# Windowed attention and two MLPs on one core: the opening's weight work behind the attention rows, a scale step tied to its join, and one wide block a gap earlier

## The chip, the cores and the metric

The kernel runs on one core of a Trainium2 chip. TensorE (PE) multiplies matrices, ScalarE (ACT) and VectorE (DVE) read its results and write its operands, GpSimd (POOL) and SyncE (SP) issue transfers, and POOL also computes a little. Each engine works through its own list of instructions in the order in which the program wrote them. The metric is the device time of one execution in microseconds (us).

## The reference, cut to what matters

```python
# windowed attention: B=4, H=8, S=768, D=64; 8 memory rows in k and v
for c in range(S // 32):                       # chunks of 32 queries
    k_full = concat([mem_k, k[l_start:r_end]]) # window: 16 left, 32, 8 right
    scores = scale * q_c @ k_full.T ; a = softmax(scores)
    out[chunk] = a @ concat([mem_v, v[l_start:r_end]])
x = out as 3072 tokens x 512
# first MLP:   h = x @ w_in (512 x 2048); g = max(0.01*h, h); y = g @ w_out
# second MLP:  h = y @ w_in2; P = a0 + a1 h + a2 h^2 + a3 h^3
#              Q = 1 + |b0||h| + |b1| h^2; out = (P / (Q + 1e-6)) @ w_out2
```

The MLP inputs come as 64-bit floats. The kernel reads each as two 32-bit words, joins them to one 32-bit float, and multiplies in split form: a number is a high half and a low half, and a product is three matmuls (high by high, high by low, low by high).

## The kernel before, in words

Tokens go in six tiles of 512 through each MLP layer. The middle dimension of 2048 is cut into 16 slices of 128, so each layer has 96 items (tile, slice). An item is 12 matmuls into a bank `hps` (`emit_h`, L596, three for each of four pieces of the inner dimension), an eviction on ACT that applies the leaky function twice (`gh` L606, `s` L607), a subtraction on DVE (`gl`, L609), and 12 matmuls into `acc` (`emit_y`, L654). A round c of the main loop first emits `hps` of item c+3 and its eviction, then the `acc` matmuls of item c; attention work stands in the two gaps behind these. So the eviction `gh` of item n is followed on PE by the `acc` matmuls of item n-3 and then by `hps` of item n+1.

A weight slice comes as a "half": one for `w_in` ("i") and one for `w_out` ("o") of each slice, in the order i0, i1, i2, o0, i3, o1, i4 and so on. A half goes through a load (SP, L121 or L124), a scale (ACT, L133), a join (three DVE instructions L147, L150, L154) and a split: a cast to the high half `wih` or `woh` (ACT, L165) and the low half `wil` or `wol` (DVE, L168, called `lower`). While the first tile is multiplied, `weights0` does this twice in a round: its first call stands behind `gh` and `s` of the round and has `gl` put into the middle of its join, its second call stands in the second gap. Three raw buffers `wr` hold loaded halves.

In the opening, the eight attention blocks of the first tile go through stages that overlap: `att_a` (transposes of q and k on PE, copies on ACT), `att_b1` (scores `pss` and their maxima `mx` on DVE), `att_e` (exp on ACT), `att_b2` (sum, reciprocal, scaling `pm` on DVE), `att_c` (transposes `pst`, copies `pb` on ACT) and `att_d` (`psx`, then `xh` on ACT and `xl` on DVE). The second tile's eight blocks are cut into pieces that `attend` spreads over the rounds of the first tile; their exp is four instructions with a row sum (L324). The later tiles use a wider form of block with a plan of slots (`wide_plan`, two slots a round). No scheduler reorders anything; the order of the code is the order on each engine.

Of the kernel before, what the change touches and what calls it, by code (L numbers as in the profile page):

```python
# [16 lines left out]
P = 128  # L17
QB = 64
LCTX, RCTX, CHUNK = 16, 8, 32
# [5 lines left out]
def kernel(  # L25
# [23 lines left out]
    nc = tc.nc  # L49
    B, H, S, D = q.shape  # L50
    NM = mem_k.shape[2]
# [118 lines left out]
    def weights0(between=()):  # L170
        if n_split[0] < FC * 2:
            lower = split_w()
            scale_w(FC * 2)
            join_w(FC * 2, between)
            lower()
            load_w(FC * 2)
        else:
            for fn in between:
                fn()
# [47 lines left out]
    qr, qT, kT, pm = {}, {}, {}, {}  # L227
    in_mem = {}

    def load_kv(j, src, mem, kind, spans):  # L230
        bi, blk = divmod(j, BPS)
        t = rooms[kind][place(kind, j)]
        c0 = blk * QB - LCTX
        for row, at, n, is_mem in spans:
            if is_mem:
                if in_mem.get((kind, place(kind, j), row)) != bi:
                    in_mem[kind, place(kind, j), row] = bi
                    nc.sync.dma_start(out=t[row:row + n], in_=mem[bi].rearrange("h p d -> p h d"))  # L238
            else:
                lo, hi = max(c0 + at, 0), min(c0 + at + n, S)  # L240
                row += lo - c0 - at
                nc.sync.dma_start(out=t[row:row + hi - lo], in_=src[bi, :, lo:hi, :].rearrange("h p d -> p h d"))
# [4 lines left out]
        nc.sync.dma_start(out=t, in_=q[bi, :, blk * QB:blk * QB + P, :].rearrange("h p d -> p h d"))  # L247
        qr[j] = t

    def load_k(j):  # L250
        load_kv(j, k, mem_k, "k", ((0, 0, NM, True), (NM, 0, CTX, False), (NM + CTX, 0, NM, True)))

    def load_qk(j):
        if j >= NB:
            return
        if j % 2 == 0:
            load_q(j)
        load_k(j)

    def load_v(j):  # L260
        if j < NB:
            W = WIN - NM
            load_kv(j, v, mem_v, "v", ((0, 0, NM, True), (NM, 0, W, False),
                                       (SB, CHUNK, W, False), (SB + W, 0, NM, True)))

    def att_bank(j, name):

# [254 lines left out]
    def wide_plan():  # L522
        def put(slot, *fns):
            wide_at.setdefault(slot, []).extend(fns)
        n0 = WIDE_FROM * NMAX // P
        last = NT // P - 1
        base = 2 * FC * (WIDE_FROM - 1)
        at = {j: base - 7 + 8 * (j - n0) for j in range(n0, last + 1)}
        at[n0], at[n0 + 1], at[n0 + 2] = base - 4, base + 3, base + 10
        put(at[n0] - 7, lambda: wide_load_qk(n0))  # L530
        put(at[n0] - 5, lambda: wide_q(n0), lambda: wide_k(n0))
        put(at[n0] - 4, lambda: wide_qk(n0), lambda: wide_load_qk(n0 + 1))
        for j in range(n0, last + 1):
            u = at[j]
            put(u, lambda j=j: wide_s(j))
            put(u + 1, lambda j=j: wide_e(j))
            if j < last:
                put(u + 1, lambda j=j: wide_q(j + 1))
                put(u + 2, lambda j=j: wide_k(j + 1))
                put(u + 3, lambda j=j: wide_qk(j + 1))  # L540
            put(u + 3, lambda j=j: wide_n(j), lambda j=j: wide_load_v(j))
            put(u + 4, lambda j=j: wide_p(j))
            put(u + 5, lambda j=j: turn_in(2, j, pwT))
            put(u + 6, lambda j=j: wide_load_qk(j + 2))
            put(u + 10, lambda j=j: wide_x(j))

    def wide(slot):
        for fn in wide_at.get(slot, ()):
# [154 lines left out]
    with tc.manual_schedule():  # L703
# [3 lines left out]
        nc.vector.memset(vb[0][0:32], 0.0)  # L707
        nc.gpsimd.memset(pall, 0.0)
        load_qk(0)
        nc.vector.memset(lnb, ONE * 2.0 ** -LN_SHIFT)  # L710
        nc.vector.memset(expb, -LN_SHIFT * math.log(2.0))
        load_k(1)
        load_v(0)
        load_qk(2)
        load_w(FC * 2)
        load_v(1)
        load_k(3)
        load_w(FC * 2)
        load_v(2)
        load_q(4)  # L720
        load_v(3)
        att_a(0)
        load_k(4)

        for j in range(FIRST + 2):
            if j < FIRST:
                att_b1(j)
                if j + 1 < FIRST:
                    att_a(j + 1)
                    if j + 5 < FIRST:  # L730
                        load_k(j + 5)
                    if j == 1:
                        load_q(6)
                att_e(j)
                att_b2(j)
            if 1 <= j <= FIRST:
                att_c(j - 1)
            if j >= 2:
                att_d(j - 2)
                if j + 2 < FIRST:  # L740
                    load_v(j + 2)
            if j == 3:
                load_w(FC * 2)
                scale_w(FC * 2)
                scale_w(FC * 2)
                join_w(FC * 2)
            if j == 4:
                load_w(FC * 2)
            if j in (5, 7, 8, 9):
                weights0()  # L750
            if j == FIRST:
                load_qk(FIRST)
                load_qk(FIRST + 1)
            if j == FIRST + 1:
                load_v(FIRST)
                load_v(FIRST + 1)
                nc.sync.dma_start(out=coef[:, 0:4], in_=a.partition_broadcast(P))
                nc.sync.dma_start(out=coef[:, 4:6], in_=b.partition_broadcast(P))

        issued_h = [0]  # L760

        def advance_h(upto):
            while issued_h[0] < min(upto, len(items)):
# [12 lines left out]
                if issued_h[0] == len(items):  # L776
                    rational(c + 1, False, True)

        wide_plan()
        advance_h(LA)  # L780
        weights0()
        for c in range(len(items)):
            layer, i, f = items[c]
            if layer == 0:
# [17 lines left out]
            if layer == 0 and i + 1 < WIDE_FROM:  # L802
                n0, n1 = tiles_of[0][i + 1]
                lastb = (n0 + n1) // QB - 1
                firstb = n0 // QB
                p0, p1 = block_end.get(firstb - 1, 0), block_end[lastb]
                span = FC - LA - 2
                start = p0 + (p1 - p0) * min(2 * f + 1, 2 * span) // (2 * span)
                end = p0 + (p1 - p0) * min(2 * f + 2, 2 * span) // (2 * span)
            look = LA if c + LA < NA else LB  # L810
            early = f == FC - 1
            if not early:
# [59 lines left out]
```

## Time and profile before

| | |
|---|---|
| median of 3 runs | 1165.43 us (1165.14 to 1165.69) |
| the profiled execution | 1165.79 us, span 1164.0 us |
| mean granted TensorE clock | 0.994 |
| busy: PE, DVE, ACT, POOL | 1135.2, 776.6, 637.2, 222.6 us |
| PE's sequence of `hps` starts | item 0 at 47.68 us |

The span is the time from the first to the last instruction in the trace; the execution is 1.79 us longer. A timeline row has the start, the duration, the engine, the line, the operation, the tiles, and in brackets how long the engine sat idle before it and what ended that.

### The profile page before, as it was taken

The numbers are of one execution on the slowest core, as the hardware profiler recorded it, in microseconds if no ns is written. First come the engines' busy times: TensorE is split into PE (matmuls) and PEld (weight loads), VectorE is DVE, ScalarE is ACT, GpSimd is POOL, SyncE is SP. The second block draws the span as 40 slices with busy tenths as digits, with TensorE's granted clock in tenths as the row PEclk, the third lists the DMA queues.
The fourth block names the chain that finished last, engine by engine and source line by source line (L and its number), as shares of the span: only waits on it lengthen the run. The fifth ranks groups of instructions, "written<-read, shape, count | busy, mean of one in ns | idle before, by whom it ended". The sixth has DMA issues, their size and how long they took to land.

```text
span 1164.0 us, 19701 instructions
## 1 busy us (share of the span) xinstructions
PE 1135.2 (98%) x7552; PEld 927.8 (80%) x7552; DVE 776.6 (67%) x1388; ACT 637.2 (55%) x1195; POOL 222.6 (19%) x255
## 2 busy tenths in 40 slices
PE   6699999999999999999999999999999999999998
PEld 4577778878887887888888888888888888888887
DVE  3788865555455554554234888788788788788775
ACT  4577742223223223223344877777777777777765
POOL 0000121132112231121000222222222222222222
PEclk9799999999999999999999999999999999999999
DMA  8677797879777787852432200200200200200000
GB/s 177 152 186 199 178 243 190 220 221 244 196 207 226 201 220 205 229 156 69 134 127 91 91 1 1 73 1 1 73 1 1 73 1 1 73 1 1 37 1 37
DMA packets 148593, 132.00 MB, mean 113 GB/s; under 512 B 63416, under 2 KB 119064, under 8 KB 148500
## 3 DMA queue, kind: packets, MB, share of 16 engines
q1 hardware_dynamic: 143635, 123.30, 37.8%
q0 software_dynamic: 4864, 7.45, 2.9%
q8 instruction: 60, 0.98, 0.4%
q14 instruction: 34, 0.27, 0.1%
HBM read 92.93 MB, written 37.75 MB: 112 GB/s over the span
## 4 chain that ended last, share of the span: by engine, by line
PE 92%; ACT 2%; DVE 2%; DMA 2%; SPq 1%; issue 1%; ACTq 0%; DVEq 0%
PE hps L596 45%; PE acc L692 22%; PE acc L654 21%; PE psx L507 2%; PE pss L465 1%; DMA kb<-in_k_dram 1%; SPq L238 1%; ACT pb L347 1%; DVE ww L150 0%; DMA qr<-in_q_dram 0%; DMA vb<-in_v_dram 0%; DVE ww L154 0%; PE pss L299 0%; ACT pm L324 0%; PE psk L284 0%
## 5 line engine op out<-in xcount | busy, mean ns | idle before, releaser
L632 POOL TENSOR_TENSOR gl<-R,gh 128x512 fp32r<-128x512 f32 x96 | 124.0, 1292 | 504.0 <-ACT gh L631 461.7
L606 ACT ACTIVATE gh<-hps 128x512 fp32r<-128x512 f32 x96 | 57.4, 598 | 292.6 <-PE hps L596 292.4
L609 DVE TENSOR_TENSOR gl<-s,gh 128x512 fp32r<-128x512 f32 x96 | 66.4, 691 | 186.4 <-ACT s L607 186.4
L596 PE MATMUL hps<-xh,wih 128*128 128x512 f32 x384 | 154.7, 403 | 3.1 <-ACT xh L515 1.8
L596 PE MATMUL hps<-xl,wih 128*128 128x512 f32 x384 | 151.1, 394 | 1.3 <-DVE xl L364 1.3
L596 PE MATMUL hps<-xh,wil 128*128 128x512 f32 x384 | 150.7, 392 | 0.4 <-DVE wil L168 0.4
L654 PE MATMUL acc<-gh,woh 128*128 128x512 f32 x384 | 151.0, 393 | 0.0
L654 PE MATMUL acc<-gh,wol 128*128 128x512 f32 x384 | 149.7, 390 | 0.0
L654 PE MATMUL acc<-gl,woh 128*128 128x512 f32 x384 | 149.5, 389 | 0.0
L596 PE MATMUL hps<-yh,wih 128*128 128x512 f32 x384 | 149.4, 389 | 0.0
L596 PE MATMUL hps<-yl,wih 128*128 128x512 f32 x384 | 149.4, 389 | 0.0
L596 PE MATMUL hps<-yh,wil 128*128 128x512 f32 x384 | 149.4, 389 | 0.0
L692 PE MATMUL acc<-woh,gh 128*128 128x512 f32 x384 | 149.4, 389 | 0.0
L692 PE MATMUL acc<-wol,gh 128*128 128x512 f32 x384 | 149.4, 389 | 0.0
L692 PE MATMUL acc<-woh,gl 128*128 128x512 f32 x384 | 149.4, 389 | 0.0
L430 POOL DMA_DIRECT2D vb<-in_v_dram x128 | 83.5, 654 | 262.1 <-PE psx L507 206.2
L619 ACT ACTIVATE A<-hps 128x512 f32<-128x512 f32 x96 | 57.1, 595 | 114.0 <-PE hps L596 113.9
L635 DVE SCALAR_TENSOR_TENSOR A<-A,small,pb 128x512 f32<-128x512 f32 x96 | 72.0, 750 | 56.3 <-ACT pb L620 56.2
L596 PEld LDWEIGHTS hps<-xh,wih 128*128 128x128 f32 x384 | 72.5, 189 | 20.3 <-ACT xh L515 2.3
L626 DVE SCALAR_TENSOR_TENSOR A<-A,pb 128x512 f32<-128x512 f32 x96 | 66.4, 692 | 30.2 <-ACT pb L639 30.2
L596 PEld LDWEIGHTS hps<-xl,wih 128*128 128x128 f32 x384 | 72.6, 189 | 17.0 <-DVE xl L364 1.8
L596 PEld LDWEIGHTS hps<-xh,wil 128*128 128x128 f32 x384 | 72.5, 189 | 16.1 <-DVE wil L168 0.8
(102 smaller groups left out, 2019.5 us busy)
## 6 DMA issues: line engine op xcount, KB each, us to landing
wr<-in_moe_w_in_dram SPq DMA_DIRECT2D x32, 512.0 KB
wr<-in_moe_w_out_dram SPq DMA_DIRECT2D x32, 512.0 KB
park_dram<-pb SPq DMA_DIRECT2D x16, 512.0 KB
pb<-park_dram SPq DMA_DIRECT2D x64, 128.0 KB
w_dram<-ww SPq DMA_DIRECT2D x32, 256.0 KB
wb<-w_dram SPq DMA_DIRECT2D x32, 256.0 KB
vb<-in_v_dram POOLq DMA_DIRECT2D x118, 56.0 KB, 3.4
kb<-in_k_dram SPq DMA_DIRECT2D x59, 112.0 KB
```

The costliest lines, as they stand in the source:

```text
L238: nc.sync.dma_start(out=t[row:row + n], in_=mem[bi].rearrange("h p d -> p h d"))
L430: nc.gpsimd.dma_start(out=vw[r + at:r + at + n, c], in_=v[bi, hs, lo:lo + n, :].rearrange("h p d -> p h d"))
L507: nc.tensor.matmul(ps[hh][e * 64:e * 64 + 64, i, c * CHUNK:(c + 1) * CHUNK], vw[r, c, 2 * i + e, :], pt[r, c, 2 * i + e, :], start=True, s ...
L596: nc.tensor.matmul(ps[:, :n], w_[:, ws], x_[:, kk, :], start=(kk == 0 and m == 0), stop=(kk == KC - 1 and m == 2))
L606: nc.scalar.activation(out=gh, in_=ps, func=AF.Prelu, alpha=0.01)
L609: return [lambda: nc.vector.tensor_tensor(out=gl, in0=s, in1=gh.bitcast(F32), op=ALU.subtract)]
L619: nc.scalar.activation(out=A, in_=ps, func=AF.Square)
L626: nc.vector.scalar_tensor_tensor(out=A0, in0=A0, scalar=ONE, in1=U0, op0=ALU.add, op1=ALU.mult)
L632: nc.gpsimd.tensor_tensor(out=gl, in0=R0, in1=gh.bitcast(F32), op=ALU.subtract)
L635: nc.vector.scalar_tensor_tensor(out=A, in0=A, scalar=babs[:, 1:2], in1=U, op0=ALU.mult, op1=ALU.add)
L654: nc.tensor.matmul(acc[i][d][:, :n], w_[:, ws], g_, start=(f == 0 and m == 0), stop=(f == FC - 1 and m == 2))
L692: nc.tensor.matmul(acc[i][s], g_[:, ss], w_, start=(f == 0 and m == 0), stop=(f == FC - 1 and m == 2))
```

## The change

The change has four parts.

1. In the opening, the loads of the first three weight halves move from between the attention rows to behind them, their scales and joins move behind the maxima of the last blocks, and one split fewer is done before the main loop. The stages of a round of the opening stand in another order (`att_d` of two blocks ago and then `att_b2`, where it was `att_b2` first). Twelve transfers of memory rows go from SP's queue to POOL's.
2. `weights0` scales only where no scaled half is waiting for its join.
3. The second tile's attention pieces begin one round later and end in the same round.
4. In the plan of wide blocks, `wide_x` of the last block of a tile stands nine slots behind the block's start, not ten.

```diff
     def weights0(between=()):
         if n_split[0] < FC * 2:
             lower = split_w()
-            scale_w(FC * 2)
+            if n_scale[0] == n_join[0]:
+                scale_w(FC * 2)
             join_w(FC * 2, between)
             lower()
             load_w(FC * 2)
...
-            put(u + 10, lambda j=j: wide_x(j))
+            put(u + (9 if j % TB == TB - 1 else 10), lambda j=j: wide_x(j))
...
         load_qk(0)
+        load_k(1)
+        for j in range(4):
+            load_v(j, what=(True,), eng=nc.gpsimd)
+            if j > 1:
+                load_k(j, what=(True,), eng=nc.gpsimd)
...
-        load_k(1)
         load_v(0)
         load_qk(2)
-        load_w(FC * 2)
         load_v(1)
         load_k(3)
-        load_w(FC * 2)
         load_v(2)
         load_q(4)
-        load_v(3)
         att_a(0)
         load_k(4)
+        load_v(3)
+        def next_w():
+            join_w(FC * 2)
+            load_w(FC * 2)
+            scale_w(FC * 2)
...
                 att_e(j)
-                att_b2(j)
-            if 1 <= j <= FIRST:
-                att_c(j - 1)
             if j >= 2:
                 att_d(j - 2)
                 if j + 2 < FIRST:
                     load_v(j + 2)
-            if j == 3:
+            if j < FIRST:
+                att_b2(j)
+            if 1 <= j <= FIRST:
+                att_c(j - 1)
+            if j in (3, 4, 5):
                 load_w(FC * 2)
+            if j == FIRST - 2:
                 scale_w(FC * 2)
-                scale_w(FC * 2)
-                join_w(FC * 2)
-            if j == 4:
-                load_w(FC * 2)
-            if j in (5, 7, 8, 9):
-                weights0()
+            if j == FIRST - 1:
+                next_w()
             if j == FIRST:
-                load_qk(FIRST)
...
+                split_w()()
             if j == FIRST + 1:
...
+                next_w()
...
+        for n in range(2):
+            split_w()()
+            next_w()
+        advance_h(1)
+        split_w()()
+        next_w()
...
         advance_h(LA)
-        weights0()
...
-                span = FC - LA - 2
+                skip = 1 if i == 0 else 0
+                span = FC - LA - 2 - skip
```

In the listings below, a number behind a name tells one use of a tile from the next.

On DVE at the end of the opening, before: `sm` and `pm` belong to the last block's softmax, `xl` to the tokens of blocks 5 and 6, `ww` to a weight half that is joined.

```order
L333 TENSOR_SCALAR sm_557<-sm_557 128x4
L334 RECIPROCAL sm_557<-sm_557 128x4
L335 TENSOR_TENSOR pm_83<-pm_83,sm_557 128x256
L364 TENSOR_TENSOR xl_285<-psx_569,xh_284 128x4x64
L147 TENSOR_SCALAR ww_477<-ww_477 128x512
L150 SCALAR_TENSOR_TENSOR ww_477<-wr_350,ww_477 128x512
L154 SCALAR_TENSOR_TENSOR ww_477<-wr_350,ww_477 128x512
L168 TENSOR_TENSOR wil_581<-ww_354,wih_580 128x512
L364 TENSOR_TENSOR xl_285<-psx_598,xh_284 128x4x64
L147 TENSOR_SCALAR ww_583<-ww_583 128x512
```

Behind `xl` of block 5 stands a whole join, and behind that a low half.

And on DVE at the same place now, from the last block's maxima to the last `xl`.

```order
L367 TENSOR_TENSOR xl_269<-psx_539,xh_268 128x4x64
L335 TENSOR_REDUCE sm_550<-pm_83 128x4
L336 TENSOR_SCALAR sm_550<-sm_550 128x4
L337 RECIPROCAL sm_550<-sm_550 128x4
L338 TENSOR_TENSOR pm_83<-pm_83,sm_550 128x256
L147 TENSOR_SCALAR ww_516<-ww_516 128x512
L150 SCALAR_TENSOR_TENSOR ww_516<-wr_346,ww_516 128x512
L154 SCALAR_TENSOR_TENSOR ww_516<-wr_346,ww_516 128x512
L367 TENSOR_TENSOR xl_269<-psx_569,xh_268 128x4x64
L168 TENSOR_TENSOR wil_588<-ww_516,wih_587 128x512
L367 TENSOR_TENSOR xl_269<-psx_591,xh_268 128x4x64
```

The half that is joined before the last two `xl` is now the first one of all (i0), and its low half stands directly ahead of the last `xl`; before, it was the third half's join and the second half's low half, and a fourth join and a third low half stood ahead of the last `xl`, which is two rows below this piece's end.

On ACT, the round of the first tile that evicts item 7, before: `gh` and `s` are its eviction, then come the two calls of `weights0`, each a cast (`woh`, `wih`) and a scale (`ww` from `wr`).

```order
L606 ACTIVATE gh_1204<-hps_1190 128x512
L607 ACTIVATE s_1203<-hps_1190 128x512
L165 CAST woh_1208<-ww_1099 128x512
L133 ACTIVATE ww_1211<-wr_1106 128x512
L347 COPY pb_82<-pst_1220 64x2x2x32 x4
L363 CAST xh_986<-psx_1263 128x4x64
L286 COPY kT_1283<-psk_1278 128x416
L324 ACTIVATE pm_83,sm_1286<-pss_1242,mx_1261 128x64 x4
L165 CAST wih_1291<-ww_1182 128x512
L133 ACTIVATE ww_1294<-wr_1188 128x512
```

The same round on ACT now.

```order
L610 ACTIVATE gh_1169<-hps_1155 128x512
L611 ACTIVATE s_1168<-hps_1155 128x512
L165 CAST wih_1173<-ww_1147 128x512
L133 ACTIVATE ww_1176<-wr_1041 128x512
L282 ACTIVATE qT_1190<-psq_1185 128x512
L289 COPY kT_1197<-psk_1192 128x416
L327 ACTIVATE pm_83,sm_1202<-pss_1110,mx_1129 128x64 x4
L350 COPY pb_82<-pst_1219 64x2x2x32 x4
L165 CAST woh_1226<-ww_1176 128x512
L133 ACTIVATE ww_1229<-wr_1071 128x512
```

The first call now casts `wih` from `ww_1147`, and scales `ww_1176`, and the second call casts that same `ww_1176`; before, each scaled tile had three more casts ahead of its own.

On DVE, the same round's `gl` and the half around it now (before, the same five instructions had `ww_1182`, scaled in the round before, and `wol`).

```order
L147 TENSOR_SCALAR ww_1176<-ww_1176 128x512
L613 TENSOR_TENSOR gl_1170<-s_1168,gh_1169 128x512
L150 SCALAR_TENSOR_TENSOR ww_1176<-wr_1041,ww_1176 128x512
L154 SCALAR_TENSOR_TENSOR ww_1176<-wr_1041,ww_1176 128x512
L168 TENSOR_TENSOR wil_1174<-ww_1147,wih_1173 128x512
```

`ww_1176` is what ACT scales behind `s_1168` in the listing above, and L147 on it stands ahead of `gl_1170`.

On DVE, the next round (item 8), now: `mx_1289` are the maxima that ACT's exp of that same round (`pm_83,sm_1314<-pss_1270,mx_1289`) reads, and that exp stands ahead of the second call's cast.

```order
L338 TENSOR_TENSOR pm_83<-pm_83,sm_1202 128x256
L306 MEMSET pss_1270 32x4x16 x2
L311 TENSOR_REDUCE mx_1289<-pss_1270 128x4
L367 TENSOR_TENSOR xl_1027<-psx_1291,xh_1026 128x4x64
L147 TENSOR_SCALAR ww_1341<-ww_1341 128x512
L150 SCALAR_TENSOR_TENSOR ww_1341<-wr_1183,ww_1341 128x512
L154 SCALAR_TENSOR_TENSOR ww_1341<-wr_1183,ww_1341 128x512
L168 TENSOR_TENSOR wol_1339<-ww_1258,woh_1338 128x512
```

The second call's join (`ww_1341`) and low half (`wol_1339`) stand behind these maxima here; in the round of item 7 the exp's maxima are those of the round before.

On SP in the second half of the opening's transfers, now (`xl` and `xh` name buffers that q, k and v rows are lent here, `wr` a raw weight half).

```order
L245 DMA kb_80<-in_k_dram 88x8x64
L250 DMA xl_86<-in_q_dram 128x8x64
L245 DMA xh_85<-in_k_dram 88x8x64 x2
L245 DMA vb_81<-in_v_dram 56x8x64 x4
L121 DMA wr_346<-in_moe_w_in_dram 128x4x256
L245 DMA xh_85<-in_v_dram 56x8x64 x2
L121 DMA wr_401<-in_moe_w_in_dram 128x4x256
L245 DMA xh_85<-in_v_dram 56x8x64 x2
L121 DMA wr_463<-in_moe_w_in_dram 128x4x256
```

Before, SP had `wr_114` as its 15th instruction and `wr_123` as its 22nd; now the first weight load is the 21st, behind all loads of q and k and most of v.

## Rows read from the trace of the kernel before

**Rows 1.** Windows (start:end length, busy us of each engine, granted clock, DMA share, GB/s).
```profile
40.00:50.00 10.00, 5.66 (x54) 3.99 (x55) 9.01 (x21) 7.13 (x21) 0.00 (x0) 0.50 0.24 76
60.00:100.00 40.00, 39.11 (x351) 30.99 (x353) 34.35 (x69) 30.12 (x88) 0.00 (x0) 1.00 0.77 199
```

**Rows 2.** Waits of TensorE, first 50 us (total, times, longest).
```profile
PE psk L284 <- DMA xh<-in_mem_k_dram: 2.8, 1, 2.8
...
PE psk L284 <- DMA kb<-in_k_dram: 1.2, 1, 1.2
```

**Rows 3.** VectorE timeline, opening: score maxima of four blocks (start, duration).
```profile
8.43 0.42 DVE L308 TENSOR_REDUCE mx<-pss 128x4 f32<-128x256 f32 x1
...
29.42 0.42 DVE L308 TENSOR_REDUCE mx<-pss 128x4 f32<-128x256 f32 x1
...
32.49 0.41 DVE L308 TENSOR_REDUCE mx<-pss 128x4 f32<-128x256 f32 x1
...
41.07 0.41 DVE L308 TENSOR_REDUCE mx<-pss 128x4 f32<-128x256 f32 x1
```

**Rows 4.** TensorE timeline, end of opening.
```profile
43.86 0.66 PE L342 MATMUL pst<-ident,pm 128*128 128x128 f32 x2 [1.38 <-DVE pm L335]
...
47.68 0.79 PE L596 MATMUL hps<-xh,wih 128*128 128x512 f32 x1 [0.83 <-ACT xh L363]
49.74 0.79 PE L596 MATMUL hps<-xl,wih 128*128 128x512 f32 x1 [1.27 <-DVE xl L364]
```

**Rows 5.** ScalarE timeline, item 7 of the first tile.
```profile
96.77 0.60 ACT L606 ACTIVATE gh<-hps 128x512 fp32r<-128x512 f32 x1 [0.45 <-PE hps L596]
...
97.74 0.62 ACT L165 CAST woh<-ww 128x512 fp32r<-128x512 f32 x1
98.25 0.69 ACT L133 ACTIVATE ww<-wr 128x512 f32<-128x512 f32 x1
...
102.14 0.32 ACT L324 ACTIVATE pm<-pss,mx 128x64 f32<-128x64 f32 x1
...
103.31 0.63 ACT L165 CAST wih<-ww 128x512 fp32r<-128x512 f32 x1
```

**Rows 6.** VectorE timeline, same item.
```profile
97.89 0.69 DVE L609 TENSOR_TENSOR gl<-s,gh 128x512 fp32r<-128x512 f32 x1 [1.08 <-ACT s L607]
98.50 0.68 DVE L150 SCALAR_TENSOR_TENSOR ww<-wr,ww 128x512 uint32<-128x512 uint32 x1
99.21 0.69 DVE L154 SCALAR_TENSOR_TENSOR ww<-wr,ww 128x512 uint32<-128x512 uint32 x1
99.82 0.69 DVE L168 TENSOR_TENSOR wol<-ww,woh 128x512 fp32r<-128x512 f32 x1
```

**Rows 7.** VectorE timeline, one attention block between two halves.
```profile
121.57 0.16 DVE L333 TENSOR_SCALAR sm<-sm 128x4 f32<-128x4 f32 x1
...
122.98 0.42 DVE L147 TENSOR_SCALAR ww<-ww 128x512 uint32<-128x512 uint32 x1
```

**Rows 8.** TensorE timeline, two matmuls of an item.
```profile
104.73 0.39 PE L654 MATMUL acc<-gh,wol 128*128 128x512 f32 x1
104.96 0.39 PE L654 MATMUL acc<-gh,woh 128*128 128x512 f32 x1
```

**Rows 9.** ScalarE timeline, evictions of items 2 and 16.
```profile
59.71 0.60 ACT L606 ACTIVATE gh<-hps 128x512 fp32r<-128x512 f32 x1 [0.54 <-PE hps L596]
...
159.68 0.60 ACT L606 ACTIVATE gh<-hps 128x512 fp32r<-128x512 f32 x1 [2.98 <-PE hps L596]
```

**Rows 10.** Waits of VectorE, 54 to 160 us.
```profile
DVE gl L609 <- ACT s L607: 11.2, 12, 3.3
```

**Rows 11.** VectorE timeline, wide transposes in item 13 to 14.
```profile
147.59 1.43 DVE L448 STREAM_TRANSPOSE pb<-kb 128x256 f32<-128x256 f32 x4 [1.15 <-DMA kb<-in_k_dram]
```

**Rows 12.** Waits of TensorE, whole span.
```profile
PE hps L596 <- ACT xh L515: 1.8, 4, 0.5
```

More of the change, by code (lines that the diff above doesn't have):

```diff
@@ L228, with load_kv @@
     in_mem = {}
-    def load_kv(j, src, mem, kind, spans):
+    def load_kv(j, src, mem, kind, spans, what=(True, False), eng=None):
         bi, blk = divmod(j, BPS)
@@ L234, in load_kv @@
         for row, at, n, is_mem in spans:
-            if is_mem:
+            if is_mem not in what:
+                pass
+            elif is_mem:
                 if in_mem.get((kind, place(kind, j), row)) != bi:
                     in_mem[kind, place(kind, j), row] = bi
-                    nc.sync.dma_start(out=t[row:row + n], in_=mem[bi].rearrange("h p d -> p h d"))
+                    (eng or nc.sync).dma_start(out=t[row:row + n], in_=mem[bi].rearrange("h p d -> p h d"))
             else:
@@ L248, in load_q, with load_k @@
         qr[j] = t
-    def load_k(j):
-        load_kv(j, k, mem_k, "k", ((0, 0, NM, True), (NM, 0, CTX, False), (NM + CTX, 0, NM, True)))
+    def load_k(j, **kw):
+        load_kv(j, k, mem_k, "k", ((0, 0, NM, True), (NM, 0, CTX, False), (NM + CTX, 0, NM, True)), **kw)
     def load_qk(j):
@@ L258, in load_qk, with load_v @@
         load_k(j)
-    def load_v(j):
+    def load_v(j, **kw):
         if j < NB:
@@ L263, in load_v @@
             load_kv(j, v, mem_v, "v", ((0, 0, NM, True), (NM, 0, W, False),
-                                       (SB, CHUNK, W, False), (SB + W, 0, NM, True)))
+                                       (SB, CHUNK, W, False), (SB + W, 0, NM, True)), **kw)
     def att_bank(j, name):
@@ L526, in wide_plan @@
         last = NT // P - 1
+        TB = NMAX // P
         base = 2 * FC * (WIDE_FROM - 1)
@@ L731 @@
                         load_k(j + 5)
-                    if j == 1:
+                    if j == 0:
                         load_q(6)
                 att_e(j)
-                att_b2(j)
-            if 1 <= j <= FIRST:
-                att_c(j - 1)
             if j >= 2:
@@ L741 @@
                     load_v(j + 2)
-            if j == 3:
+            if j < FIRST:
[3 more added lines that the diff above has]
+            if j in (3, 4, 5):
                 load_w(FC * 2)
+            if j == FIRST - 2:
                 scale_w(FC * 2)
-                scale_w(FC * 2)
-                join_w(FC * 2)
-            if j == 4:
-                load_w(FC * 2)
-            if j in (5, 7, 8, 9):
-                weights0()
+            if j == FIRST - 1:
+                next_w()
             if j == FIRST:
-                load_qk(FIRST)
-                load_qk(FIRST + 1)
+                split_w()()
             if j == FIRST + 1:
[L755 to L758, printed above, removed]
+                next_w()
         issued_h = [0]
@@ L777, in advance_h @@
                     rational(c + 1, False, True)
+        for n in range(2):
[4 more added lines that the diff above has]
+        next_w()
+        load_qk(FIRST)
+        load_qk(FIRST + 1)
+        load_v(FIRST)
+        load_v(FIRST + 1)
+        nc.sync.dma_start(out=coef[:, 0:4], in_=a.partition_broadcast(P))
+        nc.sync.dma_start(out=coef[:, 4:6], in_=b.partition_broadcast(P))
         wide_plan()
         advance_h(LA)
-        weights0()
         for c in range(len(items)):
@@ L806 @@
                 p0, p1 = block_end.get(firstb - 1, 0), block_end[lastb]
-                span = FC - LA - 2
-                start = p0 + (p1 - p0) * min(2 * f + 1, 2 * span) // (2 * span)
-                end = p0 + (p1 - p0) * min(2 * f + 2, 2 * span) // (2 * span)
+                skip = 1 if i == 0 else 0
+                span = FC - LA - 2 - skip
+                start = p0 + (p1 - p0) * max(0, min(2 * (f - skip) + 1, 2 * span)) // (2 * span)
+                end = p0 + (p1 - p0) * max(0, min(2 * (f - skip) + 2, 2 * span)) // (2 * span)
             look = LA if c + LA < NA else LB
```

## The prediction

> **What bounds the kernel now.** I read the windows first. Between 60 and 100 us, in the first tile, TensorE is busy 39.11 of 40 us and VectorE 34.35 [rows 1]: TensorE sets the time there, and VectorE has little left. Between 40 and 50 us TensorE is busy only 5.66 of 10 at a granted clock of 0.50, half of full speed, 1.2 of 2.4 GHz [rows 1]. So there are two stretches to ask about: the opening, where TensorE waits, and the first tile's rounds, where it hardly waits but VectorE is nearly full. Then the waits and the timelines of these two. In the opening TensorE waits for k rows, 2.8 us once and 1.2 us once [rows 2], and VectorE is the chain: the score maxima of four blocks stand at 8.43, 29.42, 32.49 and 41.07 us [rows 3]. The second of the three steps among these, 3.07 us, has no weight work between; 32.49 to 41.07 is two blocks with one join and one low half in them. The opening ends where the second matmul of item 0 starts, 49.74 us [rows 4]. From the eviction of item 2 (59.71) to that of item 16 (159.68) there are 14 rounds in 99.97 us [rows 9], 7.14 each.
>
> **The opening: about -11.4 us.** What goes from VectorE's path ahead of the last xl is three joins and two low halves, and the loads of weights no longer stand ahead of k rows. Steps with nothing between them take 3.07 [rows 3]; one xl now stands in the bubble behind the subtraction of the maxima, which I count as 0.1, so 3.2 a step. The first maxima at 8.43 stay. Seven steps later, 8.43 + 22.4 = 30.8, the last maxima are there, taken as 31.0 (before: 41.07). From these maxima to the transposes pst it was 43.86 - 41.07 = 2.8 us, from pst to item 0's first matmul 47.68 - 43.86 = 3.8 [rows 3, 4]. That gives 37.6; in these 3.8 us VectorE does one join and one low half, 0.42 + 0.71 + 0.61 + 0.69 = 2.4 us by like instructions [rows 6, 7], so they are covered. The last xl takes about another 0.7, so the second matmul starts at 38.3: 49.74 - 38.3 = 11.4. Another way round: three joins of 1.74 and two low halves of 0.69 are 6.6, the two DMA waits 4.0, together 10.6. The ends: 4.0 if only the DMA waits go and TensorE at half clock is the next bound, 13 if each step falls to 2.95. The transfers of memory rows on POOL's queue cost nothing as long as POOL has nothing else to do there; the trace shows no such transfer on POOL in the opening, so the ends are the two just named. The next two halves' joins and low halves, 2.4 us each, stand behind the last xl; item 0's twelve matmuls take 12 x 0.23 = 2.7 us [rows 8], and more at half clock, and cover one of them.
>
> **The rounds of the first tile: about +20 us.** Here the change takes away a lead. Let T be the start of an eviction gh. Now: ACT does two evictions, 97.74 - 96.77 = 0.97, the cast 98.25 - 97.74 = 0.51, and the scale, 0.69 [rows 5], so the scaled half is ready at T+2.17. Before, that scale had been issued one call earlier and VectorE's first join instruction was done ahead of gl, which started at 97.89, T+1.12 [rows 5, 6]. Now that instruction (L147, 0.42 [rows 7]) waits for the scale, and behind it on VectorE are gl (0.61), the two others of the join (0.71 and 0.61) and the low half (0.69) [rows 6]: the low half is ready at T+2.17+0.42+0.61+0.71+0.61+0.69 = T+5.2; before, T+1.12+2.62 = T+3.7. And its user has come nearer. The split is one half less ahead: the first call now makes wih and wil of the very next item, whose third matmul needs wil. Ten of its matmuls follow, nine steps of 0.23 and one of 0.39 [rows 8], 2.5 us, so a round takes at least 5.2 + 2.5 = 7.7, where it took 7.14.
>
> Rounds with an attention block: VectorE goes on with 122.98 - 121.57 = 1.41 us of the block [rows 7], then the second call's join and low half, 2.43: T+9.05. That is wol of the next round, whose third acc matmul TensorE reaches about 0.5 us behind the next eviction, T+8.2; it waits 0.9. That leaves 0.9 less to wait for in the round behind, so two rounds stay near 15.4, 7.7 each.
>
> Rounds in which exp stands behind maxima of the same round (in the order, the rounds of items 4, 8, 9 and 10): maxima at about T+6.3, exp 103.31 - 102.14 = 1.17 [rows 5], cast and scale 1.2, join and low half 2.43: T+11.1, and about 1.2 later where the four copies pb stand between. From there ten acc matmuls 2.3, attention pieces (estimate: 7.14 - 24 x 0.23 = 1.6 in a round, of it 1.3) and an hps of 2.9: two rounds are 17.5 to 18.9, 9.1 each. These touch six rounds. Sum: 8 x 7.7 + 6 x 9.1 = 116.2. In the round of item 13 VectorE also has the wide transposes: 1.15 us of waiting and 1.43 of work [rows 11], and a pair of q of about the same size, 4 us that now stand on the path: 120.2, so 20.2 more than 99.97. A check by VectorE alone: gl waits for s 12 times, 11.2 us [rows 10]; each of these waits now lasts until the join instruction is done, T+2.6 in place of T+1.1, 1.45 x 14 = 20 us, if VectorE, 86% busy, makes up none of it. Ends: 0 if all of it is made up, 24 if every long round takes 9.45 and the ones between 7.9.
>
> The Trainium skill (Perfetto Trace Analysis, section Tensor Engine Instruction) says that ACT and VectorE are strict first-in, first-out queues. Were it otherwise, gl would pass the waiting join and a round would be 0.6 us shorter, and the sum 8 us lower; the row of gl at 97.89, with a join instruction behind it that waited for nothing of its own, agrees with the rule.
>
> The second tile's attention pieces are the same work in 11 rounds in place of 12; TensorE's share of it is the 1.6 us above, its cost beyond the sum 0 (between -1.6 and +1.6, one round's worth).
>
> **The wide blocks: -1.8 us.** Four waits of hps for the high halves of the tokens, 1.8 us together [rows 12], are at the four tiles' last blocks; one gap, half a round, is longer than the longest (0.5). They go. If the block's transposed probabilities are late at the ninth gap the same waits stand one step earlier: 0. Lower end -2.6, upper +2.
>
> **Sum.** The profiled execution is 1165.8 us (span 1164.0 and 1.8 around it): 1165.8 - 11.4 + 20.2 - 1.8 = 1172.8. The median is 0.4 lower: 1172.4. The second MLP and the later tiles are the same work and no term.
>
> **Rivals.** A, faster: the rounds absorb the new wait. TensorE has slack of neither kind, but VectorE runs behind ACT, so that by the time it comes to the join the scale may be done; then rounds cost the bare chain at most, 14 x 7.67 = 107.4, +7.4, and 1165.8 - 11.4 + 7.4 - 1.8 - 0.4 = 1159.6; with rounds unchanged 1152.2. It decides below 8.1 us a round (13.2 / 14 = 0.94 more than 7.14). For it: ACT has waits before its evictions; against: gl waited for ACT 12 times in 14 rounds, so VectorE is mostly ahead. B, the opening doesn't start earlier as it says: the memory rows through POOL land late, or TensorE at half clock holds the blocks at their old pace; only the 4.0 go: 1179.8. For it: k waits of 2.8 us exist; against: twelve small transfers leave SP. C, the clock: with waits of 1 to 3 us in TensorE's rounds the granted clock falls to 0.50, as it stands at 40 to 50 us behind the waits for VectorE [rows 1]; a round's 24 matmuls at half clock cost 5.4 more, two such rounds 10.9: 1183.3. The Trainium skill (TensorE: Matmul & The Clock Gate, section HAM oscillation) says that repeated waits between groups of matmuls can put the clock back each time; the window above is the one stretch here that agrees, and by that rule rival C is what happens. D, the terms cancel: rounds near 8.1, 1165.
>
> **Chances.** Forecast 0.58 (its own range 1168 to 1181), A 0.20, B 0.10, C 0.07, D 0.05. Range 1157 to 1183: it leaves out A with unchanged rounds and C's far side. What a measurement can tell from no change is 0.2%, 2.3 us; faster 0.20, within 0.06 (D and the near edges), slower 0.74.
>
> **What would show it.** Second matmul of item 0 near 38 us; evictions of items 2 to 16 spread over some 120 us; a new wait of VectorE's L147 for ACT's scale, in most rounds, and of TensorE's hps and acc for wil and wol, 15 to 20 us together; the waits for xh of the wide blocks gone. I am wrong if the rounds stay below 8.1 us, or if the second matmul is not before 45.

## The result and the profile after

The changed kernel takes 1177.8 us (median of 4 runs, 1176.8 to 1180.9); the kernel before took 1165.3 beside it. The ratio is 1.0112 (95% interval 1.0093 to 1.0131): slower by 12.5 us. Forecast were 1172.4 us, with a range of 1157 to 1183. The profiled execution took 1177.9 us with a span of 1176.1.

| from the two traces | before | after | difference | forecast |
|---|---|---|---|---|
| eviction of item 2 | 59.71 | 50.50 | -9.2 | -11.4 |
| items 2 to 16 | 99.97 | 124.01 | +24.0 | +20.2 |
| items 16 to 96, four last blocks | 481.43 | 478.42 | -3.0 | -1.8 |
| from item 96 to the end of the span | 522.9 | 523.2 | +0.3 | 0 |

Item 96 is the first of the second MLP.

The first row of the table on ACT, then the eviction of item 16 (columns: start, duration, engine, line, operation, tiles, and in brackets the idle time before and what ended it). These answer to [rows 9].

```profile
50.50 0.59 ACT L610 ACTIVATE gh<-hps 128x512 fp32r<-128x512 f32 x1
```

```profile
174.51 0.60 ACT L610 ACTIVATE gh<-hps 128x512 fp32r<-128x512 f32 x1 [0.23 <-PE hps L600]
```

The end of the opening on TensorE, which answers to [rows 4]: the second matmul of item 0 starts at 40.47 us, 9.3 earlier, and waits for nothing; the low half of item 0's weights and the last xl are there.

```profile
39.87 0.80 PE L600 MATMUL hps<-xh,wih 128*128 128x512 f32 x1 [0.47 <-ACT xh L366]
40.47 0.66 PE L600 MATMUL hps<-xl,wih 128*128 128x512 f32 x1
```

The score maxima on VectorE, which answer to [rows 3]: from the fifth block on a step is 3.16 us, as worked out, but from the first block to the fourth it took 9.00 to 19.83, 3.6 a step, and to the fifth another 3.60.

```profile
9.00 0.42 DVE L311 TENSOR_REDUCE mx<-pss 128x4 f32<-128x256 f32 x1
...
19.83 0.42 DVE L311 TENSOR_REDUCE mx<-pss 128x4 f32<-128x256 f32 x1
...
29.76 0.42 DVE L311 TENSOR_REDUCE mx<-pss 128x4 f32<-128x256 f32 x1
...
32.92 0.42 DVE L311 TENSOR_REDUCE mx<-pss 128x4 f32<-128x256 f32 x1
```

The round of item 7 on ACT, which answers to [rows 5]: the cast and the scale stand behind the two evictions, and the scale ends at 95.47 + 0.69 = 96.16, T+2.17 with T = 93.99. What is scaled here is cast by the very next call; before, one other cast stood between a tile's scale and its own (`wih` from `ww_1182` for `ww_1211`), not three as the text on the listings has it.

```profile
93.99 0.60 ACT L610 ACTIVATE gh<-hps 128x512 fp32r<-128x512 f32 x1 [1.51 <-PE hps L600]
...
94.96 0.62 ACT L165 CAST wih<-ww 128x512 fp32r<-128x512 f32 x1
95.47 0.69 ACT L133 ACTIVATE ww<-wr 128x512 f32<-128x512 f32 x1
```

And on VectorE, [rows 6] before: L147 has waited 1.20 us for that scale, gl stands behind it, and the low half ends at 98.47 + 0.68 = 99.15, T+5.16.

```profile
96.19 0.43 DVE L147 TENSOR_SCALAR ww<-ww 128x512 uint32<-128x512 uint32 x1 [1.20 <-ACT ww L133]
96.54 0.69 DVE L613 TENSOR_TENSOR gl<-s,gh 128x512 fp32r<-128x512 f32 x1
97.14 0.69 DVE L150 SCALAR_TENSOR_TENSOR ww<-wr,ww 128x512 uint32<-128x512 uint32 x1
97.86 0.69 DVE L154 SCALAR_TENSOR_TENSOR ww<-wr,ww 128x512 uint32<-128x512 uint32 x1
98.47 0.68 DVE L168 TENSOR_TENSOR wil<-ww,wih 128x512 fp32r<-128x512 f32 x1
100.39 0.43 DVE L147 TENSOR_SCALAR ww<-ww 128x512 uint32<-128x512 uint32 x1 [1.24 <-ACT ww L133]
```

On TensorE the third matmul of the next item, which reads that low half, starts right behind it.

```profile
99.21 0.50 PE L600 MATMUL hps<-xh,wil 128*128 128x512 f32 x1 [0.88 <-DVE wil L168]
```

In this round the late low half costs little: the round takes 7.82 us, where it took 7.64. The loss lies elsewhere. The six rounds that the prediction named as long (items 4, 5 and 8 to 11) take 60.7 us, 16.7 more than before, and the other eight 63.3, 7.4 more.

The round of item 8 on ACT, where exp (L327) stands behind maxima of the same round. T is 101.81; the maxima, at 108.12 on VectorE, are T+6.3, as forecast. Exp has waited 3.95 us for them, with the second call's cast and scale queued behind it, and L147 then waits 3.22 us for the scale.

```profile
101.81 0.60 ACT L610 ACTIVATE gh<-hps 128x512 fp32r<-128x512 f32 x1 [1.45 <-PE hps L600]
...
108.58 0.31 ACT L327 ACTIVATE pm<-pss,mx 128x64 f32<-128x64 f32 x1 [3.95 <-DVE mx L311]
...
111.39 0.67 ACT L133 ACTIVATE ww<-wr 128x512 f32<-128x512 f32 x1
```

```profile
108.12 0.42 DVE L311 TENSOR_REDUCE mx<-pss 128x4 f32<-128x256 f32 x1
...
112.09 0.43 DVE L147 TENSOR_SCALAR ww<-ww 128x512 uint32<-128x512 uint32 x1 [3.22 <-ACT ww L133]
```

All waits of VectorE and of TensorE while the first tile is multiplied (what waited, for what, total, times, longest). VectorE's wait for s is now a wait for the scale, 31.5 us; the 11.2 us of [rows 10] start at 54 us, and of them only 5.9, in 10 waits, lie in the 14 rounds. TensorE waits for low halves, 13.8 us in 11 waits (15 to 20 were forecast), and 5.6 us for the attention's pb and pm. Between the two evictions TensorE is idle for 19.9 us, where it was idle for 2.8.

```profile
DVE ww L147 <- ACT ww L133: 31.5, 25, 3.4
```

```profile
PE acc L658 <- DVE wol L168: 10.5, 8, 2.3
PE psx L357 <- ACT pb L350: 4.0, 6, 2.4
PE hps L600 <- DVE wil L168: 3.3, 3, 2.0
PE pst L345 <- DVE pm L338: 1.6, 1, 1.6
```

What such a wait does behind itself is seen in the round of item 5: after 2.08 us without work, TensorE's matmuls take 0.63 us in place of 0.39, they start 0.43 us apart in place of 0.23, and the granted clock of the 5 us around is 0.74 (columns of the window: start:end, length, busy of each engine, clock, DMA share, GB/s).

```profile
74.54 0.40 PE L658 MATMUL acc<-gl,woh 128*128 128x512 f32 x1
77.02 0.50 PE L658 MATMUL acc<-gh,wol 128*128 128x512 f32 x1 [2.08 <-DVE wol L168]
...
77.69 0.63 PE L658 MATMUL acc<-gl,woh 128*128 128x512 f32 x1
```

```profile
75.00:80.00 5.00, 2.98 (x8) 2.36 (x9) 4.28 (x8) 2.53 (x7) 0.00 (x0) 0.74 0.65 158
```

At the wide blocks the waits for xh [rows 12] are gone: in the whole span TensorE waits for an xh once, 0.5 us, at item 0.

```profile
PE hps L600 <- ACT xh L366: 0.5, 1, 0.5
```

### The profile page after: what moved, and what is told of

Its sections match the earlier page's. It is cut to its first block, busy times and chain, and to the rows that moved or that the text cites. A ratio compares the mean times of both kernels' runs of the same rounds, so it can differ in the third digit from the quotient of the medians.

```text
span 1176.1 us, 19706 instructions
## 1 busy us (share of the span) xinstructions
PE 1139.6 (97%) x7552; PEld 927.5 (79%) x7552; DVE 777.0 (66%) x1388; ACT 638.1 (54%) x1195; POOL 230.0 (20%) x267
## 4 chain that ended last, share of the span: by engine, by line
PE 90%; DVE 4%; ACT 3%; DMA 2%; issue 1%; SPq 0%; DVEq 0%; ACTq 0%
PE hps L600 42%; PE acc L696 22%; PE acc L658 21%; PE psx L510 1%; PE pss L468 1%; DVE ww L154 1%; DVE ww L150 1%; PE psx L357 0%; ACT ww L133 0%; DMA qr<-in_q_dram 0%; DMA wr<-in_moe_w_in_dram 0%; ACT pb L350 0%; ACT pm L327 0%; DVE ww L147 0%; DMA kb<-in_k_dram 0%
## 5 line engine op out<-in xcount | busy, mean ns | idle before, releaser
L658 PE MATMUL acc<-gh,wol 128*128 128x512 f32 x384 | 152.4, 397 | 10.5 <-DVE wol L168 10.5
L658 PEld LDWEIGHTS acc<-gh,wol 128*128 128x128 f32 x384 | 73.3, 191 | 29.5 <-DVE wol L168 14.1
```

The source lines that it names most:

```text
L658: nc.tensor.matmul(acc[i][d][:, :n], w_[:, ws], g_, start=(f == 0 and m == 0), stop=(f == FC - 1 and m == 2))
```

## The experiments

Twelve kernels were run beside the kernel before. "The rule" is the condition in weights0; "gh(16)" is the start of the eviction of item 16 in the run's trace (159.7 before, 174.5 after), with which the first tile ends.

**1. The rule taken out of the changed kernel.**

```diff
             lower = split_w()
-            if n_scale[0] == n_join[0]:
-                scale_w(FC * 2)
+            scale_w(FC * 2)
             join_w(FC * 2, between)
```

> The changed kernel with one edit: each call of weights0 scales the next half again, whether or not a scaled half still waits, so the scale of a half is issued one call ahead of its join. Theory (the scale's lead): VectorE's join no longer waits for a scale that stands behind this round's eviction; most of the 24 us that items 2 to 16 took longer come back. Estimate by the same step-by-step sum as for the changed kernel: 16 us less, 1161 us (1157 to 1166), items 2 to 16 in about 108 us. Rival (the split's lead): what counts is that a half is split one call later than before; then the time stays within 4 us of 1177.8. Rival (the attention pieces in 11 rounds): also within 4 us.

Measured: 1167.5 us (1165.9 to 1169.5), ratio to before 1.0014 (1.0004 to 1.0024); items 2 to 16 in 113.1 us. The rule costs the changed kernel 10.3 us by the medians and 11.4 by the two ratios; as the cause of that the rivals are out. It is less than the 16 that were expected, and the trace says where the rest went: items 4 to 16 take 15.7 us less than in the changed kernel, but items 3 to 4 take 13.2 in place of 7.9. There ACT comes to a scale whose load has not landed, and TensorE waits 4.6 us for a copy kT behind it.

```profile
63.04 0.66 ACT L133 ACTIVATE ww<-wr 128x512 f32<-128x512 f32 x1 [4.88 <-DMA wr<-in_moe_w_in_dram]
```

**2. The call of weights0 ahead of the first round put back, with the rule.**

```diff
         advance_h(LA)
+        weights0()
         for c in range(len(items)):
```

> The changed kernel with one edit: the call of weights0 ahead of the first round stands again, so every half is split one call earlier; the scale still goes in the same call as its join. Theory (the scale's lead): the join still waits for the scale in each round, VectorE still loses it: only about 5 us come back, 1173 us (1168 to 1177). Rival (the split's lead): wil and wol are no longer needed by the next matmuls, and 16 to 24 us come back: 1154 to 1162 us.

Measured: 1176.5 us, ratio 1.0093 (1.0078 to 1.0108). The time is 1.3 us less, but the two intervals overlap, and VectorE's L147 still waits 22 times, 30.6 us. So the rival, 16 to 24 us, is out. But the half of lead isn't without effect: items 4 to 16 take 6.8 us less than in the changed kernel, and items 3 to 4 take 13.2 in place of 7.9, where ACT waits 3.0 us for a load and TensorE 5.1 for the kT behind it. TensorE's waits for low halves in the 14 rounds fall from 13.8 to 2.9 us; in their place it waits 11.7 us for pb and pm, which were 5.6.

**3. Both edits.**

> The changed kernel with both edits: the unconditional scale, and the call of weights0 ahead of the first round. Theory: both leads are as before; estimate 1159 us (1152 to 1163). If the two leads are all that was lost, the opening's 9.2 and the wide blocks' 3.0 us remain and nothing else: 1153 us. If it stays above 1157, something else in the first tile costs the rest, and the attention pieces in 11 rounds are the next suspect.

Measured: 1166.5 us, ratio 1.0007 (0.9998 to 1.0016), gh(16) at 163.7. The opening's lead of 7 us at item 2 is there and is then lost at once: items 2 to 3 took 12.2 us. ACT, TensorE and SP of this run show how. SP first: behind the load of a half at 51.54 it issues the second tile's first q, k and v rows and the coefficients, and the next weight loads come at 58.83 and after.

```profile
51.54 0.33 SPq L124 DMA_DIRECT2D wr<-in_moe_w_out_dram  x1
51.92 0.43 SPq L249 DMA_DIRECT2D qr<-in_q_dram  x1
...
55.08 2.48 SPq L244 DMA_DIRECT2D vb<-in_v_dram  x4
...
58.83 0.38 SPq L121 DMA_DIRECT2D wr<-in_moe_w_in_dram  x1
```

ACT's scale then has waited 6.88 us for a load, and with it everything behind it on ACT; TensorE waits 7.04 us for a copy kT that is queued there, and starts at half clock (granted 0.50 from 65 to 70 us; 1.08 us for pss, 0.65 otherwise).

```profile
64.27 0.66 ACT L133 ACTIVATE ww<-wr 128x512 f32<-128x512 f32 x1 [6.88 <-DMA wr<-in_moe_w_in_dram]
64.83 0.58 ACT L609 ACTIVATE gh<-hps 128x512 fp32r<-128x512 f32 x1
```

```profile
67.90 1.08 PE L301 MATMUL pss<-kT,qT 64*32 64x64 f32 x32 [7.04 <-ACT kT L288]
```

**4. The rule alone, in the kernel before.**

> The kernel before with one edit: weights0 scales only where no scaled half waits for its join. Opening, splits, pieces and wide blocks are as before. Theory (the scale's lead): slower by about 16 us, 1181 us (1174 to 1187), with a new wait of VectorE's L147 for ACT's scale. Rival (the split's lead or the pieces): within 4 us of 1165.3.

Measured: 1179.6 us, ratio 1.0120 (1.0105 to 1.0135); items 2 to 16 in 113.5 us, 13.5 more than before, with opening, splits and pieces as before. The rule alone makes a kernel as slow as the whole change does. VectorE's wait is the one of the changed kernel. On TensorE it comes out elsewhere: with the split a half earlier, TensorE waits 0.3 us for low halves, and instead 9.1 us for the attention's copies pb and, in the 14 rounds, 3.1 for pm.

```profile
DVE ww L147 <- ACT ww L133: 24.7, 24, 3.2
```

```profile
PE psx L355 <- ACT pb L348: 9.1, 9, 3.1
...
PE acc L655 <- DVE wol L168: 0.3, 1, 0.3
```

**5. The attention pieces in 12 rounds again, in the changed kernel** (`skip = 0`).

> The changed kernel with one edit: the second tile's attention pieces in 12 rounds again; the scale rule stays. Theory (the rule sets the rounds, the pieces only where a dense round is met): a few us less, 1173 us (1169 to 1177). Rival (the denser pieces are the loss): 1160 us or less.

Measured: 1184.5 us, ratio 1.0156 (1.0139 to 1.0173): slower than the changed kernel by 6.7 us. Neither expectation held for the time. From item 4 on the theory's few us are there (items 4 to 16 take 106.7 us, 2.1 less), but they are lost before. The pieces now begin in the first round, where the second tile's rows have not landed: TensorE waits 5.42 us for q, and items 2 to 3 take 16.0 us in place of 7.3. The later start of the pieces is the cover that the late row loads need.

```profile
56.21 1.11 PE L280 MATMUL psq<-ident,qr 128*128 128x128 f32 x4 [5.42 <-DMA qr<-in_q_dram]
```

**6. Pieces in 12 rounds; 7. rows early; 8. both; each with both leads of the weights.**

```diff
@@ 7 and 8
             if j == FIRST:
                 split_w()()
+                load_qk(FIRST)
+                load_qk(FIRST + 1)
             if j == FIRST + 1:
                 next_w()
+                load_v(FIRST)
+                load_v(FIRST + 1)
...
@@ 6 and 8
-                skip = 1 if i == 0 else 0
+                skip = 0
```

> The changed kernel with both leads of the weights as before (unconditional scale, the extra call of weights0), and the second tile's attention pieces in 12 rounds again. With both leads alone the time was 1166.5 us, though the opening's 9.2 and the wide blocks' 3.0 us are kept; items 3 to 16 took 98.8 us against 92.8 of the kernel before. Theory (the pieces): 11 rounds in place of 12 cost these 6 us: 1160.5 us (1158 to 1163). Rival: what is left of the loss sits in the late weight loads alone: within 1.5 us of 1166.5.

> The changed kernel with both leads as before, and SP's loads of the second tile's first block rows and of the coefficients where they were before, in the opening's last two rounds, ahead of the fourth and fifth weight load; pieces in 11 rounds. With both leads alone ACT waited 6.9 us once for a weight half, whose load stood behind these rows on SP (issued 51.9 to 58.7). Theory (the queue on SP): the wait goes, 5 to 7 us less, 1160.5 us (1159 to 1163). Rival (the transfers themselves: the DMA engines were 0.87 busy from 50 to 60 us): the weights are as late as before, within 1.5 us of 1166.5.

> Both edits of the two kernels beside it: both leads, rows early, pieces in 12 rounds. Theory (three separate costs: leads 11.3, the queue on SP 6, the pieces 6): 1154 us (1152 to 1158), which would be 11 us faster than the kernel before. Rival (pieces and late loads are one and the same loss): no faster than the better of the two beside it.

Measured: 1161.8 (ratio 0.9968, 0.9957 to 0.9980), 1162.6 (0.9972, 0.9963 to 0.9983) and 1161.1 (0.9966, 0.9954 to 0.9978). Each edit alone brings 4 to 5 us, within its theory's range, but by the medians both together hardly more (0.7 us, with overlapping intervals), and the sum of 1154 was wrong. That the two are one cost, as the rival has it, is not shown: gh(16) is 159.8, 159.8 and 157.4 against 163.7 in run 3, so in the traces both together bring 6.2 us where each brings 3.8, and they act at different places. Twelve rounds make items 4 to 16 4.4 us (run 6) and 2.6 us (run 8) shorter, with 86.3 and 86.6 the pace of the kernel before (86.1); the early rows make item 4 come 2.3 and 2.7 us sooner. In run 7 ACT's one wait for a load is not gone, as its theory had it, but split: 3.6, 2.3 and 0.4 us up to 75 us. What keeps the sum from 1154 lies before item 4: item 0 is evicted 6 to 7 us earlier than before in these runs, and at item 4 nothing of that is left without the early rows (73.6 with edit 6, as before) and 2.9 and 2.7 with them (70.7, 70.9).

**9. The wide blocks alone, in the kernel before** (ninth slot in place of the tenth).

> The kernel before with one edit: wide_x of a tile's last block at the ninth slot in place of the tenth. From the two traces each of the four tiles gains 0.76 us there: 1162.3 us, 3.0 less (2.0 to 3.5). By the prediction's term it would be 1.8 less.

Measured: 1162.1 us, ratio 0.9973 (0.9964 to 0.9983), 3.5 us less: four times 0.76 within the interval, and more than the forecast's 1.8.

**10. Weight loads one round sooner, on top of 8.**

```diff
-            if j in (3, 4, 5):
+            if j in (2, 3, 4):
                 load_w(FC * 2)
-            if j == FIRST - 2:
+            if j == FIRST - 3:
                 scale_w(FC * 2)
-            if j == FIRST - 1:
+            if j in (FIRST - 2, FIRST - 1):
                 next_w()
...
         split_w()()
-        next_w()
```

> The kernel with both leads, early rows and pieces in 12 rounds, and with the first weight loads one round of the opening sooner and one join more ahead of the last block's maxima. Theory (supply: three raw buffers, whose next loads wait for joins, let the DMA engines idle from 30 to 50 us and make the weights of items 3 and 4 late): the first matmuls start some 1.8 us later, but item 4 is evicted sooner than at 70.9, and the whole is 2 to 3 us faster than the 1161.1 of the kernel without this: 1158.5 us (1157 to 1160). Rival (VectorE's chain counts): what the join costs on VectorE is lost, 1162 to 1163 us.

Measured: 1160.4 us, ratio 0.9954 (0.9939 to 0.9969). Item 0 is evicted 2.5 us later than in 8 and item 4 0.45 sooner: the later start costs nothing, so the first rounds do wait for weights, but the gain is 0.7 us where 2 to 3 were expected, and the two intervals overlap. Between the two expectations, and not settled by size.

**11. The memory rows on SP's queue again, in the changed kernel.**

> The changed kernel with the memory rows of the opening on SP's queue again, in the order of before. If the move to POOL's queue brought what the opening gained, the second matmul of item 0 is back beyond 43 us and the time near 1181 us. If the opening's gain comes from the weight work behind the attention rows, it stays near 41 us and the time within 2 us of 1177.8. The prediction put the move at nothing.

Measured: 1176.6 us, ratio 1.0098 (1.0081 to 1.0115). The second matmul of item 0 starts at 38.29 us, which is the time that the prediction had worked out, and the last maxima stand at 30.87 (worked out: 31.0); neither expectation had it come sooner than in the changed kernel. The interval of the time overlaps that of the changed kernel.

```profile
17.96 0.42 DVE L311 TENSOR_REDUCE mx<-pss 128x4 f32<-128x256 f32 x1
...
30.87 0.42 DVE L311 TENSOR_REDUCE mx<-pss 128x4 f32<-128x256 f32 x1
```

```profile
38.29 0.66 PE L600 MATMUL hps<-xl,wih 128*128 128x512 f32 x1
```

The opening's gain is thus not from the move to POOL's queue; it is from the rest of part 1, of which no run tests the weight work and the order of stages apart. What the move costs is less sure than 40.47 against 38.29 looks. The same opening with the move has 39.25, 39.58, 40.35, 40.00 and 40.80 us in runs 1, 2, 3, 5 and 6, so run 11 lies 1.0 to 2.5 us below these; and runs 10 and 12, which differ by the move alone, have 40.77 and 40.87. How it costs isn't shown either. POOL needs 0.56 to 0.74 us to issue each of these small transfers, one behind the other, and issues the last two at 8.98 (the second column is the time of the whole group). But it issues the k rows of the third and fourth block sooner than SP does in run 11 (5.77 and 8.98 against 6.29 and 9.66), while the transposes of these rows start later (12.68 and 15.85 against 11.74 and 13.97). From POOL's issue to the landing it is 4.8 to 6.0 us for k rows, which would fit.

```profile
2.26 2.42 POOL L241 DMA_DIRECT2D vb<-in_mem_v_dram  x4
...
8.98 1.18 POOL L241 DMA_DIRECT2D xh<-in_mem_k_dram  x2
```

**12. Run 10 with the memory rows on SP's queue.**

> The kernel of the run on sooner weights, with the memory rows of the opening on SP's queue. With the changed kernel that edit brought item 0's second matmul from 40.5 to 38.3 us and the time from 1177.8 to 1176.6. Theory (POOL's queue lands these rows late and each us of the opening comes through where nothing behind is bound): 1.2 to 2.2 us less than 1160.4: 1158.7 us (1158 to 1159.5). Rival (the weights of items 3 and 4 are what the first rounds wait for, so the earlier matmuls only wait longer there): within 0.7 us of 1160.4.

Measured: 1159.9 us (1157.0 to 1161.1), ratio 0.9943 (0.9930 to 0.9957), the fastest of all by its median, 5.5 us below before; its interval overlaps that of run 10. The rival's time holds, but not its reason: the second matmul of item 0 comes at 40.87 us, no earlier than in run 10 (40.77), so there were no earlier matmuls that could wait. Item 4 is evicted at 70.53, after 70.44. ACT's waits for loads in its first rounds are 8.9 us:

```profile
ACT ww L133 <- DMA wr<-in_moe_w_out_dram: 5.7, 1, 5.7
ACT ww L133 <- DMA wr<-in_moe_w_in_dram: 3.2, 2, 1.9
```

**The runs side by side.** Item 4 divides the first tile: up to it the runs differ by what lands late, behind it by the edits. Run 9 has the first tile of before.

| kernel | eviction of item 4 | items 4 to 16 |
|---|---|---|
| before | 73.56 | 86.1 |
| changed | 65.65 | 108.9 |
| 1, rule out | 69.81 | 93.2 |
| 2, split a half earlier | 70.96 | 102.1 |
| 3, both | 72.96 | 90.7 |
| 4, rule alone | 75.17 | 99.6 |
| 5, changed, 12 rounds | 74.60 | 106.7 |
| 6, both and 12 rounds | 73.55 | 86.3 |
| 7, both and rows early | 70.68 | 89.2 |
| 8, all three | 70.89 | 86.6 |
| 10, weights sooner | 70.44 | 86.6 |
| 11, memory rows on SP | 63.48 | 108.9 |
| 12, run 10 with memory rows on SP | 70.53 | 86.3 |

Behind item 4 the account closes: 22.7 us were lost, and with the rule out, the split's lead back and 12 rounds (run 6) all but 0.1 are back. The rule is 11.4 to 15.7 of them (run 3 against 2, run 1 against the changed kernel), the split's lead 2.5 to 6.8 (run 3 against 1, run 2 against the changed kernel), the 11 rounds 2.1 to 4.4 (runs 5, 8 and 6); the shares depend on which is put right first.

## Why the prediction was right, point by point

- **The side and the mechanism.** The scale behind the round's own eviction makes VectorE's join wait, and with it gl and the low half: shown by the rows of item 7 (T+2.17 and T+5.16, forecast T+2.17 and T+5.2), by run 4 (the rule alone, +13.8 us) and by run 1 (without it, -10.3). How it reaches TensorE was only in part as forecast: through the low halves in the changed kernel, but in runs 2 and 4, where every half is split one call earlier, through the attention's pb and pm.
- **The rounds, +20.2 forecast, +24.0 measured.** The term was mis-sized by 3.8: the six rounds forecast as long took 60.7 us for 54.6, the eight others 63.3 for 65.6 (61.6 and the 4 for the wide transposes), so a part cancels. Rival C came true in pieces: the granted clock fell in three stretches, near 77, 117 and 164 us, in each of which eight steps from matmul to matmul were 0.2 us longer, 4.6 us together (from 77.69 to 81.09, 114.96 to 118.34 and 162.74 to 166.10). That would cover the miss if none of it were waited for anyway; the prediction had the clock as a rival and at nothing in the sum. The other half of the argument, the user that came nearer, is 2.5 to 6.8 us behind item 4. The argument against rival A was misread: of the 12 waits of gl in [rows 10] 10 lie in the 14 rounds, and 5.9 of the 11.2 us.
- **The pieces, cost 0 forecast (between -1.6 and +1.6).** This step failed: 11 rounds cost 2.1 to 4.4 us behind item 4, and the later start still saves 6.7 us in the changed kernel (run 5), by waiting for rows that the change has made late; where the leads are restored it costs 4.7 us (run 6 against run 3). The prediction didn't price the move of the second tile's first row loads behind the weight loads, and didn't ask who waits for them.
- **The opening, -11.4 forecast, -9.3 measured at the second matmul.** The sum held to 0.1 us with the memory rows on SP (38.29, run 11), which is in part luck, as the same opening's second matmul spreads over 1.5 us from trace to trace. Of the 2.1 us missed the likely part is the move of these rows, a cost the prediction put at nothing and named in rival B (rows that land late): 1.0 to 2.5 us in the changed kernel, nothing between runs 10 and 12. What in the move costs them stays open. The Trainium skill (DMA: Bandwidth & Descriptors, section Issuing engines are not separate DMA queues) says that issuing on several engines only saves the time of issue; no run here shows a gain from it, and run 11 starts sooner without it (38.29 against 40.47).
- **The wide blocks, -1.8 forecast, -3.0 in the traces, -3.5 alone.** Mis-sized: the prediction counted the wait, 0.46 in a block, and not the slow restart behind it. In the trace of before the matmul behind the wait of 0.46 starts at 254.62 and the two next at 255.08 and 255.42; these two steps take 0.80, otherwise 0.46, so the restart is 0.34. Wait and restart are 0.80 a block, and 0.73 to 0.77 were gained in each of the four.

```profile
254.62 0.50 PE L596 MATMUL hps<-xh,wih 128*128 128x512 f32 x1 [0.46 <-ACT xh L515]
255.08 0.50 PE L596 MATMUL hps<-xl,wih 128*128 128x512 f32 x1
255.42 0.39 PE L596 MATMUL hps<-xh,wil 128*128 128x512 f32 x1
```

- **Where the opening's gain goes.** Not foreseen: even with everything else as before, the 7 to 9 us hardly come through. Runs 3, 6, 7, 8, 10 and 12 end the first tile between 163.7 and 156.8, against 159.7. The first three weight loads are issued at 25.45, 26.97 and 30.21 us (before, the first at 8.13), and three raw buffers allow a next load only behind a join: the seventh and eighth go at 48.48 and 51.65, no earlier than before (48.81 and 52.58), though item 0 is evicted 7.7 us earlier. The DMA engines were busy 0.55 of the time from 30 to 50 us in the changed kernel, and 0.46 before. ACT's waits for loads, up to 6.9 us, are shown. That more raw buffers would cure it is argued, not shown; it wasn't tried.
- **The total.** Forecast was +7.1 from the median before, measured +12.5. The three terms were off by +2.2, +3.8 and -1.2 in the traces, and the end by +0.3, so 5.1 of these 5.4 us are named.

## What to carry to other kernels

Where engines work in order, an instruction's lead is counted in calls: ask of each producer what stands ahead of it on its own engine in that call, since a step that only looks redundant (here a scale with one half already in hand) may be the one that keeps the other engine from waiting. Work taken out of an opening must still be supplied: follow its loads, the buffers that free the next ones, and everything that was moved behind them on the same queue. And test parts alone: here one slot in a plan gave 3.5 us by itself, where the best kernel of all is 5.5 faster, and the condition on the scale cost 10 to 14.

## What the runs showed of the hardware that was not expected

In the changed kernel a single wait of 2.08 us amid otherwise dense matmuls was followed by matmuls at half clock (0.63 us each in place of 0.39, granted clock 0.74 in the 5 us around it). The length of the wait doesn't tell it: behind waits of 1.75 us (at 114.63) and 2.31 us (at 162.15) the clock fell as well, and behind 1.59 (at 107.85), 1.96 (at 136.01), 1.97 (at 55.10) and 2.39 us (at 126.11) the matmuls took 0.39 us. What decides is not shown. And twelve small transfers of 8x8x64 took 0.56 to 0.74 us each to issue on POOL, one behind the other, where SP took 0.27 to 1.02 us in run 11; in the changed kernel the fourth and fifth block's maxima stand 1.9 and 2.0 us later than there.
